# Value casts moved from the transfers to the engines, and a denser first attention, in an attention and gated-MLP kernel

## The chip, the cores and the metric

The kernel runs on one core of a Trainium2 chip. The metric is the device time of one execution in microseconds (us), as a median of several; the time of the kernel before is the median of three executions. The profile is of one execution of the same program, whose span of 335.5 us counts from the first to the last instruction.

The core's engines run side by side, each through its own queue in program order: TensorE (PE in the profile, with its weight loads as PEld), VectorE (DVE), ScalarE (ACT), GpSimd (POOL), and SyncE (SP), which here only issues DMA transfers. GpSimd issues transfers too.

## The reference

Eight heads of attention with a narrow causal mask, then a two-layer gated MLP over the result. The input sizes are 8 batches, 8 heads, 576 positions and 64 dimensions per head; the MLP goes from 512 to 2048 and back to 512.

```python
scores = q @ k.T / 8
# heads 0..3 (plain):   0 <= i - j < 32
# heads 4..7 (dilated): 0 <= i - j < 128 and (i - j) % 4 == 0
attn = softmax(where(mask, scores, -1e9)) @ v

x = attn.transpose(0, 2, 1, 3).reshape(8 * 576, 512)
h = x @ w_in                       # 512 -> 2048
g = h * sigmoid(beta * h)
out = g @ w_out                    # 2048 -> 512
```

All inputs are float32 in device memory, and so is the output; the kernel computes its matmuls in bfloat16.

## The kernel before

The work is a list of named steps, which a static schedule threads between the matmuls of the MLP. The MLP works on nine tiles of 512 tokens; while tile `t` is in work, the attention of batch `t + 1` is spread among its matmuls. Batch 0 has nothing to hide behind: its attention comes first, in the order of the list `FIRST`.

The steps, `x` being a pair of heads (0 and 1 plain, 2 and 3 dilated) and the second digit a part of the sequence:

- `Kx`, `Qx` transpose keys and queries of a pair on TensorE and copy the result from PSUM to SBUF. They are used for batches 0 and 1. From batch 2 on a DMA transpose does this, and `d`, `k`, `q` are the copies that spread its result.
- `Sxj` computes scores, and ScalarE the exp of them into `pt`; `Vxj` multiplies by the values and VectorE divides by the sums into `xs`; `Xxj` transposes that, and ScalarE copies it into `xT`, from which the MLP reads its tokens.
- `vn` brings values into the form with a one behind each row (`vd` for the dilated heads; `vp` holds the plain ones).
- `zn` writes zeros, `Hn` is the first half of an MLP block, and `Wn` is n matmuls of 512 columns on zeros, which compute nothing.

```python
FIRST = (
    "W10 K2 W2 Q2 W2 K3 S20 S21 Q3 W1 S22 S23 z0 S30 S31 S32 S33 v0 W2 V20 V21 K0 v1 W1 V22 K1 V23 W1 Q0 "
    "V30 W1 V31 W1 X20 S00 V32 S01 V33 X21 S02 S10 X30 S11 V00 S12 X31 V01 H0 X00 V10 H1 X01 V11 X10 X11 "
    "z1 z2"
).split()
```

Values come by DMA from GpSimd's queue, which turns float32 into bfloat16 on the way. The plain ones land in place, the dilated ones in a staging tile of two buffers, from which a bfloat16 copy spreads them:

```python
vp = [const([P, 4, NI, DV], BF16, f"vp{i}") for i in range(2)]
vd = [const([P, 2, 4, C, DV], BF16, f"vd{i}") for i in range(2)]
vd_st = [const([P, 2, 4, C * D], BF16, f"vd_st{i}") for i in range(2)]
# ... (cut)
def load_vp(b, eng, n=0, m=4 * NI, p=0):
    st = vp[b % 2][:].rearrange("p h i d -> p (h i) d")
    for e in range(2):
        eng.dma_start(out=st[64 * e + p:64 * e + 64, n:n + m, 0:D], in_=...)   # cut

def spread_v(b, hf, eng):
    K = DK[hf]
    copy_on(eng)(
        out=vd[b % 2][0:K, hf].rearrange("p h T e -> p (h T) e")[:, :, 0:D],
        in_=vd_st[b % 2][0:K, hf].rearrange("p h (T d) -> p (h T) d", T=C))
```

PSUM tiles of the attention rotate over four banks (`at`), and in the first attention every third over the two of `h_ps` as well. A bank is free for its next user when its reader (exp, a copy or a division) is done. The copies of a `Q` step on plain heads, and an MLP block:

```python
for n, hf in ((0, 0), (1, 1), (0, 1), (1, 0)):
    # ... (cut: out is a half of the query tile)
    copy_on(nc.scalar if hf or b == 0 and x == 0 and n else nc.vector)(out=out, in_=tv[n][rows])
# ... (cut)
def slot_h(t, fb, kts=None):
    # ... (cut: PSUM tile)
    for kt in kts or (2, 3, 0, 1):
        nc.tensor.matmul(hps, lhsT=w_in_bf[:, kt, fb * P:(fb + 1) * P],
                         rhs=xT[:, kt, t * NTOK:(t + 1) * NTOK], start=(kt == 2), stop=(kt == 1))
    # ... (cut)
    nc.scalar.activation(out=tnh[:], in_=hps, func=ACT.Tanh, scale=beta_half[:, fb:fb + 1])
    nc.vector.scalar_tensor_tensor(out=g[:], in0=tnh[:], scalar=1.0, in1=hps, op0=ALU.add, op1=ALU.mult)
```

Where each batch's next values are fetched and spread (V is VectorE, A ScalarE, G GpSimd, SQ SyncE's queue; `at(step, ...)` puts the call ahead of that step of batch `b`):

```python
if b == 1:
    at("X20", gate, raw[2, "q"][0:1, 0:1])
    at("X20", load_vp, b + 1, G)
    at("X10", spread_v, b + 1, 0, A)
    at("X11", spread_v, b + 1, 1, A)
if b > 1:
    # ... (cut: cast_qk)
    at("X20", load_vd, b + 1, G)
    at("X20", load_vp, b + 1, G)
    # ... (cut: DMA transposes, spread_dil)
    at("X00", spread_v, b + 1, 0, G)
    at("X01", spread_v, b + 1, 1, G)
```

`gate` is a copy of one element on GpSimd that holds its queue until the last transposed queries of batch 2 are there. GpSimd also multiplies the exps by the masks from batch 2 on.

Of the kernel before, what the change touches and what calls it, by code (L numbers as in the profile page):

```python
# [23 lines left out]
    "W10 K2 W2 Q2 W2 K3 S20 S21 Q3 W1 S22 S23 z0 S30 S31 S32 S33 v0 W2 V20 V21 K0 v1 W1 V22 K1 V23 W1 Q0 "  # L24
    "V30 W1 V31 W1 X20 S00 V32 S01 V33 X21 S02 S10 X30 S11 V00 S12 X31 V01 H0 X00 V10 H1 X01 V11 X10 X11 "
# [3 lines left out]
    "K2 Q2 K3 Q3 v0 S20 S21 v1 S22 S23 K0 K1 S30 V20 S31 Q0 V21 S32 V22 S33 V23 V30 S00 "  # L29
    "V31 X20 S01 V32 S02 V33 S10 X21 S11 V00 X30 S12 V01 X31 V10 X00 V11 X01 X10 X11"  # L30
).split()
THIRD = (
    "d0 d1 S20 S21 S22 k0 S23 V20 S30 k1 V21 S31 q0 V22 S32 q1 V23 S33 q2 q3 V30 X20 S00 V31 "
    "S01 X21 V32 S02 V33 S10 V00 X30 S11 V01 S12 X31 V10 X00 V11 X01 X10 X11"
# [4 lines left out]
def kernel(  # L39
# [83 lines left out]
    vd_st = [const([P, 2, 4, C * D], BF16, f"vd_st{i}") for i in range(2)]  # L123
# [24 lines left out]
    def zeros():  # L148
# [7 lines left out]
        nc.vector.memset(vp[0][0:WIN, 0, 0, 0:D], 0.0)  # L156
# [142 lines left out]
    def load_vp_1(b, eng, n=0, m=4 * NI, p=0):  # L299
        eng.dma_start(  # L300
            out=vp[b % 2][:].rearrange("p h i d -> p (h i) d")[p:P, n:n + m, 0:D],
            in_=bass.AP(tensor=v.tensor, offset=v[b, 0].offset + (QT * n - WIN + p) * D,
                        ap=[[D, P - p], [QT * D, m], [1, D]]))


    def load_vp(b, eng, n=0, m=4 * NI, p=0):
        st = vp[b % 2][:].rearrange("p h i d -> p (h i) d")
        for e in range(2):
            eng.dma_start(
                out=st[64 * e + p:64 * e + 64, n:n + m, 0:D],  # L310
# [4 lines left out]
    def load_vd(b, eng):  # L315
        rows = v[b, 4:8].rearrange("h (t T) d -> t h (T d)", T=C)
        for hf in range(2):
            eng.dma_start(out=vd_st[b % 2][0:DK[hf], hf], in_=rows[DO[hf]:DO[hf] + DK[hf]])  # L318

    def spread_v(b, hf, eng):  # L320
        K = DK[hf]
        copy_on(eng)(  # L322
            out=vd[b % 2][0:K, hf].rearrange("p h T e -> p (h T) e")[:, :, 0:D],
            in_=vd_st[b % 2][0:K, hf].rearrange("p h (T d) -> p (h T) d", T=C))

# [42 lines left out]
    def step_q(b, x):  # L368
        tv = [transposes_p("q", y) for y in (x, x + 1)] if x < 2 else transposes_d("q", x)
        h = slice(2 * (x - 2), 2 * (x - 2) + 2)  # L370
        for n, hf in ((0, 0), (1, 1), (0, 1), (1, 0)):
# [3 lines left out]
            copy_on(nc.scalar if hf or b == 0 and x == 0 and n else nc.vector)(  # L375
# [94 lines left out]
    BRING = {"d": spread_dil, "k": spread_k, "q": spread_q, "v": spread_v, "z": zeros_q}  # L470

    def attention_step(b, name):
# [3 lines left out]
        elif name[0] == "H":  # L476
            early[0] = -1
            slot_h(0, int(name[1:]), (2, 3))
        elif name[0] in STEP:
            STEP[name[0]](b, *[int(c) for c in name[1:]])  # L480
        else:
            BRING[name[0]](b, int(name[1:]), nc.vector)

# [91 lines left out]
    def extras(b):  # L575
# [4 lines left out]
        if b + 1 < B:  # L580
            if b == 1:
                at("X20", gate, raw[2, "q"][0:1, 0:1])
                at("X20", load_vp, b + 1, G)
                at("X10", spread_v, b + 1, 0, A)
                at("X11", spread_v, b + 1, 1, A)
            if b > 1:
                for kind in "kq":
                    at("S20", cast_qk, b + 1, kind)
                at("X20", load_vd, b + 1, G)
                at("X20", load_vp, b + 1, G)  # L590
# [5 lines left out]
            if b > 1:  # L596
                at("S11", spread_dil, b + 1, 0, V)
                at("V01", spread_dil, b + 1, 1, V)
                at("X00", spread_v, b + 1, 0, G)
                at("X01", spread_v, b + 1, 1, G)  # L600
# [23 lines left out]
    build_neg_p()  # L624
    load_vp_1(0, G, 2 * NI, 2 * NI)
    for c0, c1 in ((0, 256), (256, 512), (512, 1024), (1024, 2048)):
        load_w_in(c0, c1)
    make_identity(nc, ident_f[:])
    for name in FIRST:
        if name == "X10":  # L630
            build_beta()
        attention_step(0, name)
    for x, g in ((1, 0), (0, 1)):
        for n in "kq":
            load_tok(1, n, x)
        load_w_out(g)
    load_vd(1, G)
# [8 lines left out]
    load_vd(2, G)  # L646
# [7 lines left out]
    WORK = {"S": 3, "V": 3, "X": 2, "d": 3, "K": 3, "Q": 3, "k": 0, "q": 0, "v": 0}  # L654
# [64 lines left out]
```

The softmax here doesn't subtract the row's maximum and nothing guards it: scores larger than these inputs give would overflow.

## Time and profile before

| what | value |
|---|---|
| time, median of 3 (lowest to highest) | 337.47 us (337.26 to 337.99) |
| span of the profiled execution | 335.5 us, granted TensorE clock 0.99 in the mean |
| first attention up to the first MLP block that runs without a break | 0 to 27.9 us |
| transfers from GpSimd's queue | 37440 packets, 19.66 MB |
| transfers from SyncE's queue | 34224 packets, 16.53 MB |

The profile names engines by the short names given above. A line of a group or of the timeline gives source line, engine, operation, output and inputs by tile name, shapes, and how many; in the timeline the first two numbers are start and duration in us, and square brackets at the end hold the idle time of the engine ahead of the piece and what ended it. The tenths of the page's second part divide the span into 40 slices of 8.4 us, and a digit is the busy share of a slice; `PEclk` is the granted share of TensorE's clock. A busy TensorE is not always one at its peak: at half clock it is busy for twice as long with the same work.

### The profile page before, as it was taken

What the parts mean: (1) busy time and instruction counts of PE and PEld (TensorE: products, weight loads), DVE (VectorE), ACT (ScalarE), POOL (GpSimd) and SP (SyncE); (2) the same over time, 40 slices, a digit from 0 to 9 for tenths busy, and PEclk for the clock granted to TensorE, in tenths of its full rate; (3) what the DMA queues carried; (4) which work ended last, traced back from release to release, by engine and by line L of the source; (5) the groups of instructions that cost most, each with busy time, mean ns of one, the idle gap of its engine ahead of it and who ended that gap; (6) DMA issues with size and microseconds to landing.
All of it is one profiled execution on the core that took longest, in us unless ns stands there. A gap on an engine that the chain in (4) does not pass through costs nothing.

```text
span 335.5 us, 6366 instructions
## 1 busy us (share of the span) xinstructions
PE 317.6 (95%) x2426; PEld 169.1 (50%) x2426; DVE 194.3 (58%) x433; ACT 197.4 (59%) x380; POOL 141.1 (42%) x192
## 2 busy tenths in 40 slices
PE   8898999778799899999999999999999999999995
PEld 3664465434455455555554555555555544444444
DVE  4658765349665775786378637773776344344400
ACT  3577755766556665766566656665666544355511
POOL 8933494324674735564556445743533100000000
PEclk9969999999999999999999999999999999999999
DMA  6999999994949794989489959891011201011132
GB/s 87 172 210 194 201 201 163 153 211 95 114 73 191 128 120 102 158 144 97 84 168 153 98 96 178 139 90 39 25 31 33 60 26 42 32 33 31 31 92 66
DMA packets 71695, 36.60 MB, mean 109 GB/s; under 512 B 55008, under 2 KB 66288, under 8 KB 71280
## 3 DMA queue, kind: packets, MB, share of 16 engines
q0 software_dynamic: 37440, 19.66, 49.2%
q1 hardware_dynamic: 34224, 16.53, 22.8%
q8 instruction: 19, 0.31, 0.4%
q14 instruction: 12, 0.10, 0.1%
HBM read 39.32 MB, written 16.52 MB: 166 GB/s over the span
## 4 chain that ended last, share of the span: by engine, by line
PE 82%; DVE 10%; ACT 4%; DMA 1%; issue 1%; POOL 0%; DVEq 0%; ACTq 0%; POOLq 0%
PE h_ps L496 30%; PE o_ps L534 26%; PE at L534 5%; DVE g L506 4%; PE at L436 4%; PE at L496 3%; PE at L453 3%; ACT tnh L503 2%; PE at L403 2%; DVE qq L293 2%; PE h_ps L534 2%; DVE xs L443 2%; PE at L410 2%; DMA xT<-in_k_dram 1%; PE at L351 1%
## 5 line engine op out<-in xcount | busy, mean ns | idle before, releaser
L506 DVE SCALAR_TENSOR_TENSOR g<-tnh,h_ps 128x512 bf16<-128x512 bf16 x130 | 88.8, 684 | 92.5 <-ACT tnh L503 92.0
L496 PE MATMUL h_ps<-xT,w_in_bf 128*128 128x512 bf16 x520 | 130.9, 379 | 3.8 <-ACT xT L459 2.2
L503 ACT ACTIVATE tnh<-h_ps,beta_half 128x512 bf16<-128x512 f32 x130 | 89.3, 687 | 55.5 <-PE h_ps L496 52.6
L534 PE MATMUL o_ps<-w_out_bf,g 128*128 128x512 bf16 x448 | 112.8, 379 | 0.0
L496 PEld LDWEIGHTS <-w_in_bf 128*128 128x128 bf16 x576 | 51.7, 97 | 53.9 <-issue 5.6
L534 PEld LDWEIGHTS <-g 128*128 128x128 bf16 x560 | 50.4, 97 | 47.6 <-issue 0.2
L418 POOL TENSOR_TENSOR pt<-pt,mask_d 96x384 bf16<-96x384 bf16 (+1 forms) x48 | 37.0, 781 | 56.1 <-ACT pt L416 55.5
L416 ACT ACTIVATE pt<-at 128x384 bf16<-128x384 f32 (+2 forms) x107 | 46.2, 439 | 22.2 <-PE at L403 10.9
L443 DVE TENSOR_TENSOR xs<-at,rcp 48x256 bf16<-48x256 f32 (+2 forms) x91 | 42.1, 463 | 9.1 <-PE at L453 4.9
L418 POOL TENSOR_TENSOR pt<-pt,mask_PP 128x384 bf16<-128x384 bf16 x24 | 22.7, 947 | 33.4 <-ACT pt L416 33.3
L436 PEld LDWEIGHTS <-pt 128*128 128x128 bf16 (+2 forms) x448 | 24.7, 99 | 15.1 <-DVE vd L322 1.7
L539 ACT ACTIVATE osb<-o_ps 128x512 f32<-128x512 f32 x28 | 16.7, 597 | 18.6 <-PE o_ps L534 18.5
L410 PEld LDWEIGHTS <-kdT 128*96 128x96 bf16 (+1 forms) x128 | 14.3, 120 | 11.5 <-issue 2.1
L439 DVE RECIPROCAL rcp<-at 48x4 f32<-48x4 f32 (+2 forms) x91 | 16.0, 176 | 6.0 <-PE at L436 5.2
L534 PE MATMUL at<-w_out_bf,g 128*128 128x512 bf16 x80 | 19.4, 379 | 0.0
L453 PEld LDWEIGHTS <-xs 96*128 96x128 bf16 (+1 forms) x224 | 13.7, 97 | 10.9 <-issue 2.3
L453 PE MATMUL at<-ident_b,xs 96*128 96x96 bf16 (+1 forms) x224 | 18.5, 201 | 0.7 <-ACT xT L459 0.5
L436 PE MATMUL at<-vd,pt 96*128 96x65 bf16 (+1 forms) x244 | 17.6, 195 | 0.9 <-DVE vd L322 0.9
L410 PE MATMUL at<-qzd,kdT 128*80 128x96 bf16 (+1 forms) x122 | 17.1, 226 | 1.4 <-DVE qzd L281 1.4
L403 PE MATMUL at<-qq,kz 128*128 128x96 bf16 x144 | 12.1, 206 | 3.6 <-DVE qq L293 3.6
L318 POOL DMA_DIRECT2D vd_st<-in_v_dram x16 | 11.2, 702 | 10.1 <-DMA w_in_bf<-in_moe_w_in_dram 6.9
L467 ACT COPY xT<-at 128x384 bf16<-128x384 bf16 (+1 forms) x32 | 12.7, 395 | 3.8 <-PE at L453 3.8
(113 smaller groups left out, 269.7 us busy)
## 6 DMA issues: line engine op xcount, KB each, us to landing
qk<-in_k_dram POOLq DMA_DIRECT2D x6, 576.0 KB, 7.3
qk<-in_q_dram POOLq DMA_DIRECT2D x6, 576.0 KB, 10.0
vp<-in_v_dram POOLq DMA_DIRECT2D x13, 192.0 KB, 6.9
w_out_bf<-in_moe_w_out_dram POOLq DMA_DIRECT2D x4, 512.0 KB, 17.2
out_dram<-osb SPq DMA_DIRECT2D x7, 256.0 KB, 2.8
out_dram<-osb SPq DMA_DIRECT2D x8, 224.0 KB, 2.4
vd_st<-in_v_dram POOLq DMA_DIRECT2D x8, 192.0 KB, 4.1
out_dram<-osb SPq DMA_DIRECT2D x8, 192.0 KB, 2.3
```

The costliest lines, as they stand in the source:

```text
L403: nc.tensor.matmul(sc[:, a, h2 * n:(h2 + 1) * n], lhsT=kz[b % 2][:, h4, i].rearrange("p e u -> p (e u)"), rhs=qq[b % 2][:, h4, i].rearrang ...
L410: nc.tensor.matmul(sc[0:K, a, 0:2 * n], lhsT=kd[b][:, rp, h4, DO[hf]:DO[hf] + K], rhs=qzd[b % 2][:, :, rp, h4, hf * DQ[0]:hf * DQ[0] + n], ...
L416: nc.scalar.activation(out=w, in_=sc[0:K, :, 0:2 * n], func=ACT.Exp, scale=SCALE)
L418: nc.gpsimd.tensor_tensor(out=w, in0=w, in1=mask[0:K], op=ALU.mult)
L436: nc.tensor.matmul(pv[:, a, h2, :], lhsT=pt[x][0:K, c:c + P], rhs=rhs, start=True, stop=True)
L443: nc.vector.tensor_tensor(out=xs_t[b, x, jx][:, a0:a0 + m], in0=pv[0:n, :, :, 0:D], in1=rcp[0:n, 0:m].unsqueeze(3).to_broadcast([n, m, 2, ...
L453: nc.tensor.transpose(xp[:, a * n:(a + 1) * n], xs[:, a].rearrange("p h d -> p (h d)"), ident_b[0:n, 0:n])
L496: nc.tensor.matmul(hps, lhsT=w_in_bf[:, kt, fb * P:(fb + 1) * P], rhs=xT[:, kt, t * NTOK:(t + 1) * NTOK], start=(kt == 2), stop=(kt == 1))
L503: nc.scalar.activation(out=tnh[:], in_=hps, func=ACT.Tanh, scale=beta_half[:, fb:fb + 1])
L506: nc.vector.scalar_tensor_tensor(out=g[:], in0=tnh[:], scalar=1.0, in1=hps, op0=ALU.add, op1=ALU.mult)
L534: nc.tensor.matmul(ops[:], lhsT=g_t[t, fb][:, tb * P:(tb + 1) * P], rhs=w_out_bf[:, fb, :], start=(fb == 0), stop=(fb == NFB - 1))
L539: nc.scalar.mul(out=osb[:], in_=ops[:], mul=0.5)
```

## The change

It does three things.

1. Values are no longer cast by the transfer. All of them land as float32 in staging tiles (`vp_st`, `vd_st`, the latter now one buffer), and `cast_v` copies them to bfloat16 on an engine: on VectorE or GpSimd for batch 0, VectorE and ScalarE for batch 1, ScalarE for batch 2, GpSimd from batch 3 on. From batch 2 on their transfers are issued on SyncE's queue.
2. The first attention is put in another order, with fewer `W`: the transposes of plain keys and queries follow each other, the plain scores begin among the second dilated pair's values, and of Q0's four copies VectorE takes two instead of one.
3. GpSimd's queue at the start is rearranged: the mask of the plain scores and the loads of `w_in` come behind the first value cast, the last half of `w_in` behind the cast of the first plain values.

A step `v` also counts in the pacing of steps among the MLP's matmuls now, which moves a few steps by one place in the first two tiles.

```diff
 FIRST = (
-    "... v0 W2 V20 V21 K0 v1 W1 V22 K1 V23 W1 Q0 "
-    "V30 W1 V31 W1 X20 S00 V32 S01 V33 X21 S02 S10 X30 S11 V00 S12 X31 V01 H0 X00 V10 H1 X01 V11 X10 X11 "
+    "... v0 W2 V20 V21 v1 K0 W1 K1 V22 Q0 V23 "
+    "V30 S00 V31 X20 S01 V32 S02 V33 X21 v4 S10 X30 S11 V00 S12 X31 V01 H0 v5 X00 V10 H1 X01 V11 X10 X11 "
 SECOND = (
-    "K2 Q2 K3 Q3 v0 S20 S21 v1 S22 S23 K0 K1 S30 ... V31 X20 S01 V32 ..."
+    "K2 Q2 K3 Q3 v0 S20 v1 S21 S22 S23 K0 K1 S30 ... V31 X20 v2 S01 V32 ..."
 THIRD = (
-    "d0 d1 S20 S21 S22 k0 S23 V20 S30 ... V33 S10 V00 ..."
+    "d0 d1 v0 S20 S21 S22 k0 S23 v1 V20 S30 ... V33 v2 S10 V00 ..."
...
-    vd_st = [const([P, 2, 4, C * D], BF16, f"vd_st{i}") for i in range(2)]
+    vp_st = [const([P, 4, NI, D], FP32, f"vp_st{i}") for i in range(2)]
+    vd_st = const([P, 2, 4, C, D], FP32, "vd_st")
...
-    def spread_v(b, hf, eng):
+    def cast_v(b, n, eng):
+        if n == 2 or n > 3:
+            h = slice(0, 4) if n == 2 else slice(2 * n - 8, 2 * n - 6)
+            copy_on(eng)(out=vp[b % 2][:, h, :, 0:D], in_=vp_st[b % 2][:, h])
+        else:
+            f, K = (slice(n, n + 1), DK[n]) if n < 2 else (slice(0, 2), 96)
+            copy_on(eng)(out=vd[b % 2][0:K, f]...[:, :, 0:D], in_=vd_st[0:K, f]...)
...
-            copy_on(nc.scalar if hf or b == 0 and x == 0 and n else nc.vector)(
+            copy_on(nc.scalar if hf else nc.vector)(
...
-            BRING[name[0]](b, int(name[1:]), nc.vector)
+            eng = (nc.scalar if name[0] == "v" and (b, name) in ((1, "v2"), (2, "v0"), (2, "v1"), (2, "v2")) else
+                   nc.gpsimd if b == 0 and name in ("v1", "v4", "v5") else nc.vector)
+            BRING[name[0]](b, int(name[1:]), eng)
...
-            if b == 1:
-                at("X20", gate, raw[2, "q"][0:1, 0:1])
-                at("X20", load_vp, b + 1, G)
-                at("X10", spread_v, b + 1, 0, A)
-                at("X11", spread_v, b + 1, 1, A)
             if b > 1:
+                if b == 2:
+                    at("S20", gate, raw[2, "q"][0:1, 0:1])
                 ...
-                at("X20", load_vd, b + 1, G)
-                at("X20", load_vp, b + 1, G)
+                at("X20", load_vd, b + 1, SQ)
+                at("X20", load_vp, b + 1, SQ)
+            if b == 1:
+                at("X20", load_vd, b + 1, SQ)
+                at("X20", load_vp, b + 1, SQ)
...
-                at("X00", spread_v, b + 1, 0, G)
-                at("X01", spread_v, b + 1, 1, G)
+                at("X00", cast_v, b + 1, 3, G)
+                at("X01", cast_v, b + 1, 2, G)
...
-    build_neg_p()
     load_vp_1(0, G, 2 * NI, 2 * NI)
-    for c0, c1 in ((0, 256), (256, 512), (512, 1024), (1024, 2048)):
-        load_w_in(c0, c1)
-    make_identity(nc, ident_f[:])
     for name in FIRST:
+        if name == "v1":
+            attention_step(0, "v1")
+            build_neg_p()
+            for c0, c1 in ((0, 256), (256, 512), (512, 1024)):
+                load_w_in(c0, c1)
+            continue
+        if name == "v5":
+            load_w_in(1024, 2048)
+            make_identity(nc, ident_f[:])
...
+    G.memset(vd_st[64:96, 1], 0.0)
     load_vd(1, G)
...
-    load_vd(2, G)
...
-    WORK = {"S": 3, "V": 3, "X": 2, "d": 3, "K": 3, "Q": 3, "k": 0, "q": 0, "v": 0}
+    WORK = {"S": 3, "V": 3, "X": 2, "d": 3, "K": 3, "Q": 3, "k": 0, "q": 0, "v": 1}
```

## The prediction

> **What bounds the kernel now.** I read the page's first two parts first: which engine is busy, and when it is not.
>
> ```profile
> PE 317.6 (95%) x2426; PEld 169.1 (50%) x2426; DVE 194.3 (58%) x433; ACT 197.4 (59%) x380; POOL 141.1 (42%) x192
> PE   8898999778799899999999999999999999999995
> PEclk9969999999999999999999999999999999999999
> ```
>
> TensorE is busy for 317.6 of 335.5 us, no other engine for more than 59%. Of the idle 17.9 us, 3.8 lie behind the last matmuls and all but 0.8 of the rest before 120 us; one slice (16.8 to 25.2 us) had a granted clock of 0.6. The windows of that stretch and of two later ones (PE, PEld, DVE, ACT, POOL busy, clock, DMA share, GB/s):
>
> ```profile
> 12.00:16.00 4.00, 3.10 (x59) 2.13 (x60) 2.90 (x10) 1.28 (x2) 3.53 (x7) 0.91 2.10 162
> 16.00:20.00 4.00, 4.00 (x58) 3.03 (x57) 1.89 (x7) 2.48 (x5) 2.61 (x5) 0.50 1.40 199
> 20.00:24.00 4.00, 3.85 (x44) 2.90 (x43) 1.92 (x8) 3.13 (x9) 1.43 (x2) 0.74 1.16 213
> 60.00:70.00 10.00, 7.92 (x72) 4.32 (x69) 3.96 (x10) 7.63 (x15) 3.14 (x5) 1.00 1.17 167
> 180.00:200.00 20.00, 19.73 (x164) 10.57 (x162) 11.90 (x28) 12.50 (x25) 11.48 (x14) 1.00 0.94 106
> ```
>
> From 120 us on TensorE idles about 0.3 us per batch: three waits of 0.27 us for a query copy on VectorE are all that the timeline lists from 120 us until the last ten. So nothing that the change does to GpSimd or DMA after the third batch can save much, and only a new wait there could cost. What can move lies before 120 us. The timeline of TensorE there has these large stalls:
>
> ```profile
> 67.48 0.38 PE L496 MATMUL h_ps<-xT,w_in_bf 128*128 128x512 bf16 x1 [1.98 <-ACT xT L459]
> 72.68 0.50 PE L410 MATMUL at<-qzd,kdT 128*96 128x192 bf16 x4 [1.37 <-DVE qzd L281]
> 86.00 0.34 PE L403 MATMUL at<-qq,kz 128*128 128x96 bf16 x4 [1.49 <-DVE qq L293]
> ```
>
> What ScalarE did before the first of them:
>
> ```profile
> 64.36 0.60 ACT L539 ACTIVATE osb<-o_ps 128x512 f32<-128x512 f32 x1
> 64.86 1.03 ACT L322 COPY vd<-vd_st 96x1024 bf16<-96x1024 bf16 x1
> 65.79 0.40 ACT L459 COPY xT<-at 128x288 bf16<-128x288 bf16 x1
> 66.08 1.05 ACT L322 COPY vd<-vd_st 80x1024 bf16<-80x1024 bf16 x1
> 67.03 0.40 ACT L459 COPY xT<-at 128x288 bf16<-128x288 bf16 x1
> ```
>
> Two value copies for batch 2 stand in ScalarE's queue ahead of the last two copies into `xT`, and the next token tile's first block needs the last of these. And in the first attention, warm-up matmuls (`W`) that compute nothing stand on the path at half clock, ahead of the first plain scores:
>
> ```profile
> 17.44 0.62 PE L475 MATMUL o_ps<-warm_w 128*128 128x512 bf16 x1
> 17.85 0.43 PE L436 MATMUL at<-vd,pt 96*128 96x65 bf16 x4
> 18.09 0.62 PE L475 MATMUL o_ps<-warm_w 128*128 128x512 bf16 x1
> 18.82 0.52 PE L391 MATMUL h_ps<-neg_p,ident_b 128*128 128x384 bf16 x1
> ```
>
> **What the Trainium skill says.** "TensorE: Matmul & The Clock Gate", Part 1: the clock is gated to half after a quiet window of about 3.4 us and restored after a busy one, with windows that run free of the kernel; Part 4 adds that transposes don't count as busy in the same way. The trace agrees: 0.50 in 16 to 20 us, after four microseconds of transposes and waits, and a 128x384 matmul takes 0.52 us there against 0.33 later. "VectorE: DVE Perf Modes", Mode 2×_2P: a float32 copy within SBUF can run at two elements a cycle, where bf16 gets four. The before trace has only bf16: 96x1024 in 0.35 us undisturbed, about 1.0 while GpSimd worked. "SBUF — State Buffer", Who interferes with whom: such copies and GpSimd shut each other out of a port pair; those 1.0 us fit that. "DMA: Bandwidth & Descriptors", SWDGE vs HWDGE vs iDMA: a cast during the transfer has to be issued from GpSimd. Hence the old loads of values all stand on POOL, at 0.97 us an issue for `vp` and 0.70 for `vd_st`; float32 staging lets batches from the third on use SyncE's queue.
>
> **The change part by part.**
>
> (a) *First attention.* Four single warm-ups after V21 become one. The three that go took 0.43, 0.43 and about 0.41 us on the chain that ended last, 1.27 in all. V22 also loses its 0.49 us wait for the second value copy, since K0, one warm-up and K1 now stand ahead of it. Against that, the first value copy is float32: 1024 elements at 1.92 per ns are 0.53, plus some 0.1 fixed, so 0.62 against 0.35: +0.3. And the first plain scores must wait for query copies that come right behind Q0. With V20 at about 12.5, K0, W, K1, V22 end near 14.5 and Q0's 36 transposes, at half clock 1.5 us, near 16. ScalarE then copies (1,1) and (0,1), 0.64 each, so S00 can start at 17.2, where it was 18.8. V31 and X20 (0.22 + 0.32) are now behind S00 instead of ahead: a lead of 1.1 us at half clock. If the clock comes back at 22.2 as before, work that is 1.1 us ahead in cold time is 0.55 ahead in warm time. I count −0.6 at the start of the MoE tiles.
>
> (b) *Values of heads 0 to 3, batch 0.* They land in float32 and GpSimd casts each half, 768 elements. Its copies ran at about 1.0 ns an element (80x1024 in 1.04 us), so 0.8 us. The loads landed some 7 us after issue: 17 to 18 us, so casts end near 18.5 and 20.5; the first consumer stood at 22.7. Hidden. GpSimd's wait delays the last half of `w_in` by some 4 us in issue, but the DMA engines have a backlog until then, and its first use is past 34 us, against a landing at 28. Hidden: 0.
>
> (c) *Batch 1.* Two VectorE casts stay, in float32, about 1.0 us each as before because GpSimd works beside them: 0. One ScalarE cast of `vp` is new: 0.83 ns an element (597 ns at 512, 385 at 256) and 0.17 fixed, so 1536 elements take 1.45 us, at about 55.5 us where ScalarE is under half busy. S10 needs the bank of S01 some 2.6 us later and the exp then ends about in time: +0.1.
>
> (d) *End of batch 1.* The two copies of 1.03 and 1.05 leave ScalarE's queue. Three `xT` copies then follow the `osb` at 64.96 at 0.30 us spacing and end at 65.9, where TensorE is at the wait from 65.3 on. 1.98 us become about 0.6: −1.4.
>
> (e) *Batch 2.* Its three casts now run on ScalarE inside the second token tile. The first falls into a gap of 1.88 us: free. With the changed pacing both query copies of the dilated heads follow each other on VectorE, where a `g` of 0.60 stood between: −0.6 of the 1.37. The second cast (1.04) stands between two `tnh` in a stretch where VectorE is the tight engine and ScalarE has some 0.4 to spare: +0.5. The third, 1.45, among plain scores with TensorE 99% busy: +0.3.
>
> (f) *Batches 3 to 7.* GpSimd per batch: 2 × 0.97 + 2 × 0.70 + 2.07 = 5.4 us before; 2.05 (2048 elements) + 1.55 (1536) = 3.6 after. It was idle a good part anyway, and TensorE's order there is unchanged: 0.
>
> Sum: −0.6 + 0.1 − 1.4 − 0.6 + 0.5 + 0.3 = −1.7, so 337.5 becomes 335.8 us.
>
> **Rivals.** *First: the clock.* With fewer warm-ups a second quiet window could follow, as S00 waits for the query copies; another 3.4 us at half clock loses 1.7 us, and the gains are gone: 337.5. For it: the window from 12 to 16 was already too quiet with the warm-ups in. Against: from 18.8 on scores, values and transposes stand densely, with no idle, as before. The opposite, a clock that stays up, would save some 2 us more: 333.8. *Second: ScalarE becomes the wait in the second tile.* A `tnh` held up by 1.0 to 1.5 us holds a `g`, and that a bank of `h_ps`, of which there are two. If each of the four new casts shows in full (1.45 + 1.03 + 1.04 + 1.45 = 5.0), less (a), (d) and (e), the time is about 339.9. Against: ScalarE idles for 55.5 us ahead of its `tnh` waiting on matmuls. *Third: late staging.* The loads of batch 2 now sit behind the DMA transposes on SyncE's queue, whose last landed at 61.8; if they land after 71, a cast blocks ScalarE, with exp and `tnh` behind it: +1 to +4. Against: some ten microseconds of slack, and loads of this size landed in 4.1 us at the median. *Fourth: GpSimd's casts block VectorE's copies* in the later batches, up to 3.6 us each, and TensorE's 0.27 waits grow to about 1: +4. Against: the masks' products already run there.
>
> **Range and chances.** The parts are each uncertain by some 0.5 to 1 us and mostly independent: ±2.3. Predicted 335.8, with 333.3 to 338.2 holding 8 times in 10. To be faster by 2% it must lose 6.7 us, half of the 13.3 that all idle time before 120 us adds up to: 4%. Slower by 2% needs the second and fourth rivals at once: 4%. The rest, 92%, within.
>
> **What would show it.** Right: no value copy before the last `xT` copies of batch 1, and the wait at 67.5 under 0.8; S00 near 17.2; the dilated query wait under 0.9; idle from 120 us unchanged. Wrong: a low clock past 23 us; TensorE waits on ScalarE's `vd` or `vp` in the second tile; waits on `qq` over 0.5 us per batch later; ScalarE waiting for `vd_st`.

## The result, and the profile after

| | before | after |
|---|---|---|
| time, median | 337.38 us (4 executions) | 335.81 us (4 executions, 335.19 to 336.29) |
| ratio | | 0.9949, 95% interval 0.9927 to 0.9971 |
| span of the profiled execution | 335.5 us | 334.6 us |
| granted TensorE clock in it | 0.99 | 0.984 |
| transfers on GpSimd's queue | 37440 packets, 19.66 MB | 7632 packets, 16.64 MB |
| transfers on SyncE's queue | 34224 packets, 16.53 MB | 57264 packets, 25.58 MB |

The kernel became 1.6 us faster; 335.8 was predicted. The profile shows that this sum came about in another way than the prediction had it: one step had the wrong sign (the first attention, +1.0 for −0.6), two were put too small (a gain of 2.8 for 1.9, a loss of 0.9 for 0.5), and one that was put at nothing gained 0.7.

The page's first two parts, after (busy time of the engines; 40 slices of 8.4 us):

```profile
PE 318.5 (95%) x2423; PEld 169.6 (51%) x2423; DVE 194.8 (58%) x433; ACT 198.7 (59%) x381; POOL 131.5 (39%) x172
PE   8698999997999899999999999999999999999995
PEclk9959999998999999999999999999999999999999
```

TensorE is busy for 0.9 us more than before, with the same work less three warm-ups: part of what was won in idle time was paid back as time at half clock. The second slice has become emptier (6 where it was 8). The third has a lower clock than before (5, not 6), and there is a new dip in the tenth slice. The windows of the same stretches, after, and one more from 80 us (PE, PEld, DVE, ACT, POOL busy, clock, DMA share, GB/s):

```profile
12.00:16.00 4.00, 1.64 (x40) 1.26 (x41) 1.63 (x5) 0.68 (x2) 2.62 (x5) 1.00 1.19 199
16.00:20.00 4.00, 3.29 (x66) 2.67 (x61) 2.18 (x5) 1.91 (x4) 3.24 (x7) 0.59 1.18 174
20.00:24.00 4.00, 4.00 (x41) 3.20 (x39) 2.44 (x9) 2.76 (x7) 4.00 (x8) 0.55 1.05 160
60.00:70.00 10.00, 9.48 (x83) 5.16 (x81) 5.20 (x13) 7.21 (x16) 1.21 (x3) 1.00 1.14 203
80.00:90.00 10.00, 8.91 (x62) 4.37 (x60) 7.51 (x18) 5.08 (x10) 1.60 (x3) 0.83 0.65 137
```

From 12 to 16 us TensorE was busy for 1.64 us where it had been 3.10. From 60 to 70 us it is the reverse: 9.48 where it had been 7.92. The timeline of TensorE after, at the places that matter (start, duration, what; in brackets the idle time ahead and what ended it):

```profile
14.77 0.65 PE L358 MATMUL h_ps<-ident_b,xT 64*64 64x64 bf16 x18 [1.78 <-DMA xT<-in_k_dram]
19.71 0.48 PE L404 MATMUL at<-qq,xT 128*128 128x192 bf16 x2 [0.38 <-ACT qq L382]
28.75 0.38 PE L505 MATMUL h_ps<-xT,w_in_bf 128*128 128x512 bf16 x1 [0.27 <-ACT xT L466]
65.47 0.30 PE L460 MATMUL at<-ident_b,xs 96*128 96x96 bf16 x3 [0.52 <-DVE xs L450]
70.86 0.50 PE L417 MATMUL at<-qzd,kdT 128*96 128x192 bf16 x4 [0.76 <-DVE qzd L282]
79.46 1.02 PE L505 MATMUL h_ps<-xT,w_in_bf 128*128 128x512 bf16 x4 [1.08 <-DVE g L515]
81.36 1.65 PE L505 MATMUL h_ps<-xT,w_in_bf 128*128 128x512 bf16 x4 [0.75 <-DVE g L515]
115.33 0.34 PE L410 MATMUL at<-qq,kz 128*128 128x96 bf16 x4 [1.30 <-DVE qq L294]
```

The lines of before that go with the first, the sixth and the seventh of these:

```profile
12.82 0.65 PE L351 MATMUL h_ps<-ident_b,xT 64*64 64x64 bf16 x18 [0.23 <-DMA xT<-in_k_dram]
80.74 1.02 PE L496 MATMUL h_ps<-xT,w_in_bf 128*128 128x512 bf16 x4 [0.55 <-DVE g L506]
82.25 1.02 PE L496 MATMUL h_ps<-xT,w_in_bf 128*128 128x512 bf16 x4 [0.36 <-DVE g L506]
```

The first line is the first plain key transpose: its wait for the tokens' own transfer is now 1.78 us, where it was 0.23. The mask of the first plain scores goes in at 18.82, as before, and their product starts at 19.71 (before: 19.14). The 1.98 us for `xT` at 67.48 are gone, with 0.52 for `xs` in their place. The dilated query wait of 1.37 is 0.76. The two waits on a `g` that were 0.55 and 0.36 (at 80.74 and 82.25) are 1.08 and 0.75, and the second of these blocks falls into a stretch at half clock: 1.65 us for four matmuls instead of 1.02.

ScalarE ahead of the place where the 1.98 stood, after:

```profile
64.73 0.60 ACT L548 ACTIVATE osb<-o_ps 128x512 f32<-128x512 f32 x1 [0.47 <-PE o_ps L543]
65.23 1.00 ACT L466 COPY xT<-at 128x288 bf16<-128x288 bf16 x3
```

No value copy stands among the `xT` copies; three of them take 1.00 us together.

**The ledger.** The change was profiled twice (the second time as the repeat below), and one table of start times (us) of the same work shows where the time went:

| place | before | after | after, repeat |
|---|---|---|---|
| first MLP block without a break | 27.73 | 28.75 | 27.73 |
| dilated scores of batch 2 (waits for `qzd`) | 72.68 | 70.86 | 70.63 |
| second of the MLP blocks that wait for a `g` | 82.25 | 81.36 | 81.11 |
| plain scores of batch 3 (wait for `qq`) | 115.56 | 115.33 | 113.93 |
| end | 335.5 | 334.6 | 333.1 |

The differences from row to row are the steps' worths. After: +1.0 in the first attention, −2.8 up to batch 2's dilated scores, +0.9 at the two waits for a `g`, +0.7 from there to batch 3's plain scores, −0.7 after them: −0.9 in all. Repeat: 0, −2.05, +0.9, −0.5, −0.8: −2.4. The two executions of one program differ by 1.5 us: 1.0 in the first attention and 1.2 from 81 us on, less 0.8 the other way between them.

### The profile page after: what moved, and what is told of

The parts are those of the page before. It is cut to its first block, busy times and chain, and to the rows that moved or that the text cites. A ratio compares the mean times of both kernels' runs of the same rounds, so it can differ in the third digit from the quotient of the medians.

```text
span 334.6 us, 6370 instructions
## 1 busy us (share of the span) xinstructions
PE 318.5 (95%) x2423; PEld 169.6 (51%) x2423; DVE 194.8 (58%) x433; ACT 198.7 (59%) x381; POOL 131.5 (39%) x172
## 3 DMA queue, kind: packets, MB, share of 16 engines
q1 hardware_dynamic: 57264, 25.58, 39.8%
q0 software_dynamic: 7632, 16.64, 27.7%
## 4 chain that ended last, share of the span: by engine, by line
PE 84%; DVE 5%; ACT 3%; DMA 3%; POOL 2%; issue 1%; POOLq 0%; ACTq 0%; DVEq 0%
PE h_ps L505 31%; PE o_ps L543 28%; PE at L543 5%; PE at L443 4%; PE at L460 3%; PE at L505 3%; DMA xT<-in_q_dram 3%; DVE g L515 2%; PE at L410 2%; PE h_ps L543 2%; PE at L417 2%; ACT tnh L512 1%; PE at L559 1%; POOL pt L425 1%; DVE xs L450 1%
## 5 line engine op out<-in xcount | busy, mean ns | idle before, releaser
L450 DVE TENSOR_TENSOR xs<-at,rcp 96x256 bf16<-96x256 f32 (+2 forms) x93 | 43.0, 462 | 9.2 <-PE at L460 5.0
L446 DVE RECIPROCAL rcp<-at 96x4 f32<-96x4 f32 (+2 forms) x93 | 16.3, 176 | 8.6 <-PE at L443 8.0
L460 PE MATMUL at<-ident_b,xs 96*128 96x96 bf16 (+1 forms) x220 | 17.8, 201 | 1.5 <-DVE xs L450 1.0
L443 PE MATMUL at<-vd,pt 80*128 80x65 bf16 (+1 forms) x252 | 18.5, 197 | 0.7 <-DVE vd L329 0.7
L417 PE MATMUL at<-qzd,kdT 128*80 128x96 bf16 (+1 forms) x122 | 17.2, 227 | 0.8 <-DVE qzd L282 0.8
L425 POOL TENSOR_TENSOR pt<-pt,mask_FP 128x384 bf16<-128x384 bf16 x12 | 10.9, 911 | 17.0 <-ACT pt L423 17.0
L505 PE MATMUL at<-xT,w_in_bf 128*128 128x512 bf16 x56 | 13.8, 379 | 0.7 <-DVE kdT L371 0.4
L474 ACT COPY xT<-at 128x192 bf16<-128x192 bf16 (+1 forms) x31 | 12.2, 393 | 3.6 <-PE at L460 3.6
```

Source lines behind the costliest of these rows:

```text
L417: nc.tensor.matmul(sc[0:K, a, 0:2 * n], lhsT=kd[b][:, rp, h4, DO[hf]:DO[hf] + K], rhs=qzd[b % 2][:, :, rp, h4, hf * DQ[0]:hf * DQ[0] + n], ...
L425: nc.gpsimd.tensor_tensor(out=w, in0=w, in1=mask[0:K], op=ALU.mult)
L443: nc.tensor.matmul(pv[:, a, h2, :], lhsT=pt[x][0:K, c:c + P], rhs=rhs, start=True, stop=True)
L446: nc.vector.reciprocal(out=rcp[0:n, 0:m], in_=pv[0:n, :, :, D])
L450: nc.vector.tensor_tensor(out=xs_t[b, x, jx][:, a0:a0 + m], in0=pv[0:n, :, :, 0:D], in1=rcp[0:n, 0:m].unsqueeze(3).to_broadcast([n, m, 2, ...
L460: nc.tensor.transpose(xp[:, a * n:(a + 1) * n], xs[:, a].rearrange("p h d -> p (h d)"), ident_b[0:n, 0:n])
```

## The experiments

The kernel before ran beside each of them; its median was 337.0 to 337.2 us every time. Experiments 2, 3, 7 and 8 ran on another chip than the rest; the kernel before took 336.99 us there, and 337.0 and 337.16 on the chip of the others.

**1. The change once more.** No edit.

> The changed kernel once more, unaltered, beside the next three. Theory A (K0's tokens land later and at times that vary from one execution to the next, as float32 values stand ahead of them): K0's start anywhere from 13.6 to 14.8, time 335.4 us, ratio 0.995. Theory B (the profile shown first is typical): K0 at 14.8 again, ratio 0.995.

Measured: 335.59 us (15 executions, 333.75 to 337.67), ratio 0.995 (0.9929 to 0.9972). The same lines of the timeline:

```profile
14.12 0.65 PE L358 MATMUL h_ps<-ident_b,xT 64*64 64x64 bf16 x18 [1.41 <-DMA xT<-in_k_dram]
46.98 1.02 PE L543 MATMUL h_ps<-w_out_bf,g 128*128 128x512 bf16 x4 [0.88 <-DVE g L515]
79.22 1.02 PE L505 MATMUL h_ps<-xT,w_in_bf 128*128 128x512 bf16 x4 [1.09 <-DVE g L515]
```

The token wait is there again and varies with the transfers: 1.41 and 1.78 us. So are the waits for a `g` (1.09, then 0.74), but at 81 us the clock stays up this time. New here is 0.88 us at 46.98, which the first profile doesn't have.

The executions of both kernels fall into groups by their mean granted clock, some 0.005 apart; one stretch of 3.4 us at half clock (the profile after has one from 81.4 to 84.8, clock 0.53) makes 0.005 of a span of 335 us. All executions of the two kernels that ran as or beside experiments, by the mean clock to the nearest 0.005 (mean time, number; two of the kernel before, at 340 us, are left out):

| clock | before | after |
|---|---|---|
| 0.980 | | 336.38 (3) |
| 0.985 | 337.58 (2) | 335.54 (6) |
| 0.990 | 337.50 (74) | 334.52 (6) |
| 0.995 | 336.09 (30) | |
| 1.000 | 335.15 (8) | |

At the one clock where both have some number of executions, 0.990, the change is worth 3.0 us; at 0.985, with only two executions of the kernel before, 2.0. The medians, 335.59 against 337.0, show 1.4. So part of the gain is lost because the changed kernel gets a lower clock more often; how much, 0.6 to 1.6 us by these groups, is not measured more closely, since no experiment sets the clock alone.

**2. The new first attention alone.** The kernel before, with the change's order of steps, its copies of Q0 on two engines, its second value copy on GpSimd and its order of GpSimd's queue (but for the last half of `w_in`, which follows the rest); values are still cast by the transfer.

```diff
-    "... V20 V21 K0 v1 W1 V22 K1 V23 W1 Q0 "
-    "V30 W1 V31 W1 X20 S00 ..."
+    "... V20 V21 v1 K0 W1 K1 V22 Q0 V23 "
+    "V30 S00 V31 X20 S01 ..."
-            copy_on(nc.scalar if hf or b == 0 and x == 0 and n else nc.vector)(
+            copy_on(nc.scalar if hf else nc.vector)(
```

> The kernel before, with the new first attention alone: order, three warm-ups fewer, the copies of Q0, the second value copy on GpSimd ahead of the plain mask and w_in; values still cast by the transfers. Theory A (the order is a gain that float32 staging hides): the first unbroken MLP block at 27.1 instead of 27.7, time 336.8 us. Theory B (the order itself is what costs): 28.7 and 338.4 us. Theory C (fewer warm-ups lengthen the stretch at half clock): half clock past 23 us and 338 us or more.

Measured: 336.38 us (21 executions), ratio 0.9973 (0.9954 to 0.9993). The plain keys' transposes started at 12.68, the product of S00 at 17.30 (17.2 was predicted of the change), and the first unbroken MLP block at 26.52, 1.2 us ahead of the kernel before. So the order does what step (a) said, and more at this place; some of it goes again in a longer wait for a `g` at 45.54 (0.65 us, 0.18 before). What cancels it in the changed kernel comes with the float32 values.

**3. Batch 0's dilated values cast by the transfer again.** The changed kernel; the two loads go as bfloat16 into the same staging tile, through another view of it. VectorE and GpSimd still copy them, from that view.

```diff
+    vd_sb = vd_st[:].rearrange(...).bitcast(BF16)[:, 0:8 * C * D].rearrange(...)   # cut
-        st = vd_st[:].rearrange("p f h T d -> p f h (T d)")
+        st = (vd_st[:] if b else vd_sb).rearrange("p f h T d -> p f h (T d)")
```

> The changed kernel, with batch 0's dilated values alone cast by their transfer again (bf16 staging; everything else as changed). Theory A (the doubled bytes of these values, which stand ahead in the queue, bring K0's tokens 2 us later): K0's transposes start near 12.9 instead of 14.8, the first MLP block that runs without a break near 27.2 instead of 28.8, time 334.2 us. Theory B (the tokens are late for another reason, such as GpSimd's queue or the order of the steps): K0 still near 14.8, time 335.8 us.

Measured: 332.55 us (6 executions), ratio 0.9874 (0.9841 to 0.9906): 3 us below the change, where 1.6 was expected. The key transposes started at 12.55 with no wait for tokens, the unbroken MLP at 26.30, 1.4 and 2.4 us ahead of the change's two profiles. What lies ahead of the tokens in GpSimd's queue makes this difference. What made up the rest of the 3 us was not isolated; three of the six executions had a clock of 1.0, which none of the change's had. The view of transfers issued in the first 12 us (KB, us from issue to landing), before:

```profile
xT<-in_k_dram POOLq DMA_DIRECT2D x1, 288.0 KB, 6.0
vd_st<-in_v_dram POOLq DMA_DIRECT2D x1, 160.0 KB, 6.3
```

and after:

```profile
xT<-in_k_dram POOLq DMA_DIRECT2D x1, 288.0 KB, 7.9
vd_st<-in_v_dram POOLq DMA_DIRECT2D x1, 320.0 KB, 8.1
```

The key tokens' transfer is the same 288 KB in both, and lands 1.9 us later after its issue, because the value loads ahead of it write 384 and 320 KB instead of 192 and 160. In this experiment it landed after 5.6 us.

**4. Tokens ahead of the values.** The changed kernel; the plain tokens' loads are issued before those of batch 0's values.

```diff
-    load_vd(0, G)
-    build_neg_d()
     ... (the plain tokens' loads)
+    load_vd(0, G)
+    build_neg_d()
```

> The changed kernel, with the loads of plain keys' and queries' tokens issued ahead of batch 0's float32 values instead of behind. Theory A (what counts is how many bytes stand ahead of whom in the transfer queue): K0 no longer waits, but the values now land some 2 us later, at 14 to 15, and V20 waits for them where it stood at 12.6, so K0 waits behind V20: no gain, 335.8 us. Theory B (the tokens alone are what is late): 334.0 us.

Measured: 337.71 us (22 executions), ratio 1.0033 (1.0012 to 1.0055). The wait moved to the values: 2.99 us on `vd` ahead of V20, which then started at 14.74. With these bytes the order of the loads can't mend it: whichever comes second is late. It is 1.9 us slower than the theory expected: the clock was 0.985 or less in 20 of 22 executions, and VectorE's first cast for batch 1 (at 47.07 us) waited 1.37 us for its load, with a wait of 1.92 on TensorE behind it.

**5. Seven warm-ups in the token wait.** The changed kernel with `W7` ahead of `K0`.

```diff
-    "... V20 V21 v1 K0 W1 K1 V22 Q0 V23 "
+    "... V20 V21 v1 W7 K0 W1 K1 V22 Q0 V23 "
```

> The changed kernel with seven warm-up matmuls of 512 columns put ahead of the first plain key transposes, where TensorE waited 1.4 to 1.8 us for the tokens. Nothing else changes. Theory A (the window from 12 to 16 us is too quiet, since the tokens land late, and that is what takes the clock down at 16 us): seven cost 1.5 us at full clock, so up to 1.5 of the wait is filled for nothing and the path gets longer by at most 0.3; the clock at 16 to 20 us is then 0.9 or more, the first unbroken MLP block starts at 26.5 instead of 27.7 to 28.7, and the time is about 334.0. Theory B (the clock is taken down by the many transposes and waits after 16 us as well, whatever stands ahead): the half clock only moves, the start stays at 27.7 to 28.7, time 335.6 or up to 0.3 more.

Measured: 333.58 us (4 executions, 333.17 to 334.04), ratio 0.9893 (0.985 to 0.9936). The mean clock was 1.0 in three executions and 0.994 in the profiled one. Its windows:

```profile
12.00:16.00 4.00, 3.29 (x49) 1.81 (x48) 1.96 (x6) 1.01 (x4) 3.39 (x6) 1.00 1.20 195
16.00:20.00 4.00, 3.20 (x80) 2.56 (x75) 2.95 (x8) 2.78 (x7) 2.71 (x6) 1.00 1.26 199
20.00:24.00 4.00, 3.82 (x53) 2.76 (x53) 3.18 (x12) 3.17 (x9) 4.00 (x8) 1.00 1.23 214
```

The clock stays at 1.00 through the stretch that had 0.59 and 0.55. The warm-ups took 1.68 us, just what was waited anyway, and the first unbroken MLP block starts at 26.52: as early as in experiment 2. So 512-column matmuls put ahead of 16 us were enough to hold the clock, whatever came after it, and matmuls that compute nothing won 2.0 us. But idle time in this window is not needed for the clock to fall. In experiments 2 and 3 K0 waits for no tokens, and TensorE was busy for 3.65 and 3.80 of these 4 us, mostly with transposes and products of 65 columns. Experiment 3, and below it experiment 9 (described further down), which has the same first attention:

```profile
12.00:16.00 4.00, 3.80 (x94) 3.13 (x95) 2.57 (x9) 1.98 (x5) 3.37 (x7) 0.90 1.10 229
16.00:20.00 4.00, 3.61 (x32) 2.73 (x31) 2.76 (x10) 2.76 (x6) 3.68 (x8) 0.50 1.34 196
...
12.00:16.00 4.00, 3.60 (x94) 2.92 (x95) 2.56 (x9) 2.06 (x4) 3.43 (x7) 1.00 1.09 231
```

The clock falls in the first and stays at 1.00 in the second, up to 24 us and beyond. With this first attention it can go either way; which mixture of matmuls suffices is not settled.

**6. The three removed warm-ups put back.**

```diff
-    "... V22 Q0 V23 "
-    "V30 S00 V31 X20 ..."
+    "... V22 Q0 W1 V23 "
+    "V30 W1 S00 V31 W1 X20 ..."
```

> The changed kernel with the three single warm-ups put back, where they stood in the kernel before: one behind the first plain query transposes, one ahead of the first plain scores and one behind the third value step of the second dilated pair. Theory A (step (a) of the prediction: they lie on the path at half clock and cost what they take): 3 times 0.42 us is +1.3, of which the later end of the cold stretch gives half back, so +0.6 to +1.3 and a time of 336.2 to 336.9. Theory B (TensorE waits for late tokens and query copies there anyway, so that they fill waits, and they help the clock): 0 or a gain, 335.0 to 335.6.

Measured: 334.73 us (20 executions), ratio 0.9928 (0.9905 to 0.995). They cost nothing that shows: executions at a clock of 0.990 took 334.76 us, against the change's 334.52, and 0.990 is now the commonest clock where it was 0.985 and 0.990 in equal number. Step (a) had booked their removal as 1.27 us off the path. The profile still has a half clock at 16 to 20 us (0.50): all three stand behind 16 us. The intervals of this run and of the change overlap, so that a gain isn't shown, only that the loss of 0.6 to 1.3 us didn't come.

**7. Batch 2's value copies moved, alone.** The kernel before, with its two copies (bfloat16) taken from the end of batch 1 and put, still on ScalarE, where the change has its first and second cast.

```diff
-    "d0 d1 S20 S21 S22 k0 S23 V20 ..."
+    "d0 d1 v0 S20 S21 S22 k0 S23 v1 V20 ..."
-                at("X10", spread_v, b + 1, 0, A)
-                at("X11", spread_v, b + 1, 1, A)
```

> The kernel before, with one thing changed: batch 2's two value copies leave ScalarE's queue ahead of X10 and X11 of batch 1 and stand inside the second token tile, as in the changed kernel. Theory A (this move is where the gain comes from): the wait of 1.98 us at 67.5 falls under 0.6, some 0.5 us comes back in the second tile, time 337.4 - 1.4 = 336.0 us. Theory B (the copies only change place, and the second tile loses as much): 337.4 us. Theory C (nothing comes back): 335.6 us.

Measured: 335.97 us (22 executions), ratio 0.9975 (0.996 to 0.9991). The 1.98 us are gone, and this alone brings the two longer waits for a `g`:

```profile
79.10 1.02 PE L496 MATMUL h_ps<-xT,w_in_bf 128*128 128x512 bf16 x3 [1.08 <-DVE g L506]
80.99 1.02 PE L496 MATMUL h_ps<-xT,w_in_bf 128*128 128x512 bf16 x4 [0.75 <-DVE g L506]
```

They are the same to 0.01 us as in the changed kernel: it is the place of the copies on ScalarE that costs 0.9 us, not float32. The traces point to the way. Behind the second copy an exp comes later on ScalarE, so GpSimd's masks on it come at another time against VectorE's copies, which stand ahead of the `g`. In the kernel before:

```profile
78.11 2.10 POOL L418 TENSOR_TENSOR pt<-pt,mask_d 96x384 bf16<-96x384 bf16 x2 [1.55 <-ACT pt L416]
78.74 0.69 DVE L285 COPY kz<-kpT 64x1536 bf16<-64x1536 bf16 x1
80.61 0.45 DVE L293 COPY qq<-qpT 64x1152 bf16<-64x1152 bf16 x1
```

and in the changed kernel, where experiment 7 is alike (1.03 and 0.84):

```profile
76.82 2.10 POOL L425 TENSOR_TENSOR pt<-pt,mask_d 96x384 bf16<-96x384 bf16 x2 [2.08 <-ACT pt L423]
77.12 1.03 DVE L286 COPY kz<-kpT 64x1536 bf16<-64x1536 bf16 x1
79.33 0.83 DVE L294 COPY qq<-qpT 64x1152 bf16<-64x1152 bf16 x1
```

The two copies are 0.34 and 0.38 us longer, 0.72 of the 0.92 by which the two waits grow. The dilated query wait stayed at 1.37, so its shortening needs another part of the change.

**8. Batch 2's casts on GpSimd.** All three, ahead of the masks of the second tile.

```diff
-    "d0 d1 v0 S20 ... S23 v1 V20 ... V33 v2 S10 ..."
+    "d0 d1 v0 v1 v2 S20 ... S23 V20 ... V33 S10 ..."
-            eng = (nc.scalar if ... (2, "v0"), (2, "v1"), (2, "v2") ...          # cut
-                   nc.gpsimd if b == 0 and name in ("v1", "v4", "v5") else nc.vector)
+            eng = (nc.scalar if ... (b, name) in ((1, "v2"),) else               # cut
+                   nc.gpsimd if b == 0 and name in ("v1", "v4", "v5") or b == 2 and name[0] == "v" else nc.vector)
-                    at("S20", gate, raw[2, "q"][0:1, 0:1])
+                    at("d0", gate, raw[2, "q"][0:1, 0:1])     # and cast_qk of batch 3 likewise
```

> The changed kernel, with batch 2's three casts on GpSimd, ahead of its masks, instead of on ScalarE. Theory A (casts on ScalarE in the second tile cause TensorE's waits of 1.08 and 0.75 us near 80 and the half clock after them): waits under 0.6 each, no third stretch at half clock, mean clock 0.99, time 334.0 us. Theory B (those waits come from VectorE's kz and qq copies that stand behind GpSimd's masks): unchanged, 335.8 us. Theory C (the casts on GpSimd shut out VectorE's copies of the dilated queries): the wait of 0.76 at 70.9 grows to over 1.5, 336.5 us.

Measured: 343.13 us (6 executions), ratio 1.0184 (1.0155 to 1.0213). None of the three theories had this. GpSimd, and TensorE behind it:

```profile
77.58 1.47 POOL L326 CAST vp<-vp_st 128x1536 bf16<-128x1536 f32 x1 [8.11 <-DMA vp_st<-in_v_dram]
79.98 0.35 PE L443 MATMUL at<-vd,pt 96*128 96x65 bf16 x3 [5.97 <-POOL pt L425]
```

The plain values of batch 2 land at 77.5 us only, and with the cast at the head of an in-order queue the masks wait 8.11 us for them. This is the prediction's rival of late staging, seen from the engine that had to wait: the change itself escapes it since it puts that cast late, at `v2`.

**9. Only the two dilated casts on GpSimd.** Experiment 3, with `v0` and `v1` of batch 2 on GpSimd ahead of the masks, and the plain cast left on ScalarE.

```diff
-    "d0 d1 v0 S20 S21 S22 k0 S23 v1 V20 ..."
+    "d0 d1 v0 v1 S20 S21 S22 k0 S23 V20 ..."
-            eng = (nc.scalar if ... (2, "v0"), (2, "v1"), (2, "v2") ...
-                   nc.gpsimd if b == 0 and name in ("v1", "v4", "v5") else nc.vector)
+            eng = (nc.scalar if ... (2, "v2") ...
+                   nc.gpsimd if b == 0 and name in ("v1", "v4", "v5") or b == 2 and name in ("v0", "v1") else nc.vector)
-                    at("S20", gate, raw[2, "q"][0:1, 0:1])
+                    at("d0", gate, raw[2, "q"][0:1, 0:1])     # and cast_qk of batch 3 likewise
```

> The changed kernel, with batch 0's dilated values cast by their transfer (as in the first of these runs), and batch 2's two dilated value casts on GpSimd ahead of its masks; the plain cast of batch 2 stays on ScalarE. Theory A (the second dilated cast on ScalarE adds to TensorE's waits near 77 and 79): they fall from 1.08 and 0.75 to about 0.55 and 0.36, as in the kernel before, and nothing holds up the masks, because these two loads had landed by 69.3: 331.8 us. Theory B (the waits come from VectorE's own copies alone): 332.6 us. Theory C (a cast on GpSimd holds up the masks): a wait of V20 on pt over 1 us, 334 us or more.

Measured: 332.8 us (6 executions), ratio 0.9878 (0.9832 to 0.9925), no better than experiment 3 without it. In the timeline of TensorE the first wait for a `g` is back at its old size, and another has grown:

```profile
68.24 0.50 PE L419 MATMUL at<-qzd,kdT 128*96 128x192 bf16 x4 [1.58 <-DVE qzd L284]
76.29 1.02 PE L507 MATMUL h_ps<-xT,w_in_bf 128*128 128x512 bf16 x4 [0.54 <-DVE g L517]
```

0.54 and 0.35 us instead of 1.08 and 0.75, with the two VectorE copies at 0.69 and 0.45 again: ScalarE's casts there were behind those waits. Which of the two, no run separates; in the timeline it is the second that stands ahead of the exp. But GpSimd's casts run beside VectorE's dilated query copies (1.74 us for two, 0.92 in experiment 3), and that wait goes from 0.97 in experiment 3 to 1.58.

**10. More warm-ups on top.** Experiment 9 with seven more (`W4` after `K0`, `W4` ahead of `Q0`).

```diff
-    "... K0 W1 K1 V22 Q0 V23 "
+    "... K0 W4 K1 V22 W4 Q0 V23 "
```

> The kernel of the run before (batch 0's dilated values cast by transfer, batch 2's dilated casts on GpSimd), with seven more warm-up matmuls among the plain transposes of the first attention (four instead of one behind K0, four ahead of Q0): 7 x 0.22 = 1.5 us of TensorE's time at full clock. Theory A (dense 512-column matmuls there keep the clock up, and 6.8 us at half clock go): 331.8 + 1.5 - 3.0 = 330.3 us, no slice with a clock of 0.5. Theory B (the window is quiet anyway): 331.8 + 1.5 to 3.0 = 333.3 to 334.8 us, half clock as before.

Measured: 332.5 us (6 executions, 331.9 to 332.81), ratio 0.9857 (0.9822 to 0.9891). The clock was 0.998 or 1.0 in every one. Four of experiment 9's six were at 0.995 or more and took 331.5 to 333.2: what the clock brings in the others is used up by the warm-ups, with which the first unbroken MLP block starts at 25.65, where experiment 9's profile, at full clock without them, had 24.20.

**11. Fewer of them.** Experiment 3 with four more.

```diff
-    "... K0 W1 K1 V22 Q0 V23 "
+    "... K0 W3 K1 V22 W2 Q0 V23 "
```

> The changed kernel with the dilated values of batch 0 cast by the transfer again (as in the run that gave 332.55 us), plus four more warm-up matmuls: three instead of one between the first and second plain key transposes and two ahead of the first plain query transposes. Seven more had kept the clock at 0.998 to 1.0 in every execution and cost 1.5 us. Theory A (fewer are enough): clock 0.995 or more, the four cost 0.85 us of 2.2 that a whole half-clock stretch or so is worth, time 331.3 to 331.9. Theory B (four leave the window too quiet in most executions): clock 0.987 as without, time 332.6 to 333.4.

Measured: 332.87 us (4 executions, 332.76 to 332.97), ratio 0.9875 (0.9841 to 0.991). Four are enough for the clock (1.0 in three executions, 0.994 in one), and still no gain over experiment 3, whose executions at 1.0 took 331.9 us: the four cost the 0.9 us that they were counted at. The first theory had the clock right and the time wrong by 1 us.

**12. Later values through GpSimd's queue again.** The changed kernel; the loads of batches 3 to 7 are issued by GpSimd, still as float32.

```diff
-                at("X20", load_vd, b + 1, SQ)
-                at("X20", load_vp, b + 1, SQ)
+                at("X20", load_vd, b + 1, SQ if b == 1 else G)
+                at("X20", load_vp, b + 1, SQ if b == 1 else G)
```

> The changed kernel, but the values of batches 3 to 7 are fetched through GpSimd's queue again, still as float32 and cast there. Theory A (the three waits of 0.27 us for a query copy on VectorE at 147, 180 and 214 us went because GpSimd no longer issues transfers beside that copy): the copy takes 0.7 us again instead of 0.46, the three waits come back, and the time is 0.8 us longer, about 336.4. Theory B (they went because of another spacing of the steps, or because the value copies became GpSimd casts of another length): no such waits, time 335.6.

Measured: 335.34 us (20 executions), ratio 0.9931 (0.9909 to 0.9952). VectorE's fourth query copy of batch 4 in the changed kernel:

```profile
146.14 0.46 DVE L294 COPY qq<-qpT 64x1152 bf16<-64x1152 bf16 x1
```

and in this experiment, with TensorE behind it:

```profile
145.64 0.69 DVE L294 COPY qq<-qpT 64x1152 bf16<-64x1152 bf16 x1
...
146.39 0.34 PE L410 MATMUL at<-qq,kz 128*128 128x96 bf16 x4 [0.26 <-DVE qq L294]
```

The three waits are back (at 146, 180 and 213 us, 0.26 each), as the first theory said, with two transfers being issued on GpSimd (1.43 us from 145.33) beside the copy. The median doesn't show the 0.8 us: 335.34 against 335.59, with intervals that overlap. At a clock of 0.990 the executions took 335.03 (12) against 334.52 (6), at 0.985 336.14 (5) against 335.54 (6): some 0.5 us at equal clock.

## Why the prediction was right, and where it was not

The time fell on the predicted value by luck: errors cancelled. The mechanism of the largest step, (d), was right. By its steps:

**(a), first attention: predicted −0.6, +1.0 and 0 in the two profiles. This step failed.** "With V20 at about 12.5, K0, W, K1, V22 end near 14.5" took K0's tokens to land when they had. They came 1.3 to 2 us later, since twice the bytes stand ahead of them (experiments 2 and 3, which keep the order and take the bytes away, begin the MLP at 26.5 and 26.3). And S00, which was to start at 17.2 "where it was 18.8", had its product at 19.71 and 18.68; 18.8 was the start of its mask, and the product of before stood at 19.14. The float32 cast itself took the estimated 0.62 us. Nor did the three warm-ups lie on the path for 1.27 us: put back, they cost 0.2 at equal clock (experiment 6).

**(b), batch 0's plain values: predicted 0.** The casts were as estimated and hidden. What was missed is that GpSimd's first cast, of the second dilated half, had to wait for the late load too, 2.43 us, and that the cost lies in the bytes on this queue and not in the casts.

**(c), batch 1: predicted +0.1.** ScalarE's cast took 1.48 us and no new wait followed. But "Two VectorE casts stay, in float32, about 1.0 us each as before" holds for one profile and not the other: 0.94 us in the first, 1.71 in the repeat, where it held a `g` and TensorE for 0.88. In the repeat a memset of GpSimd ran from 44.42 to 45.79, and the cast, issued at 44.63, ended at 46.34: 0.55 after the memset. In the kernel before, one ran to 45.35 and the copy issued at 44.62 ended at 45.63. This agrees with the Trainium skill, "SBUF — State Buffer", Who interferes with whom: when a VectorE copy in a two-port mode and GpSimd overlap, the second to issue blocks until the first is done. How long such a cast takes depends on the phase against GpSimd's work, so 1.0 us was no constant. Two waits of before, 0.38 us at 58.58 and 0.18 at 46.28, are not listed after, which with (d) and the query wait of (e) makes −2.6 of the ledger's −2.8; in the repeat the 0.88 gives part of that back, and −2.05 is left.

**(d), end of batch 1: predicted −1.4, right.** 1.98 became 0.52, −1.46, by the named mechanism; experiment 7 shows it alone. (The wait began at 65.5, which is 67.48 less 1.98, and not at 65.3.)

**(e), batch 2: predicted +0.2 in all, measured −0.2 in the repeat and +1.0 in the first profile.** The dilated query wait lost 0.61 (−0.6 predicted). The second cast was mis-sized: +0.9, where +0.5 stood; experiments 7 and 9 put it on the casts' place on ScalarE, and most of it is VectorE's copies beside GpSimd's masks, which the prediction didn't count there. After it, waits of 1.49 and 0.51 gave way to 0.35 and 0.30 in the repeat, with new ones of 0.23 for the third cast (+0.3 predicted) and 0.52: −0.5 in the ledger. The +0.9 and this −0.5 are not independent: the wait of 1.49 ends with a query copy on VectorE, and TensorE, held up ahead of it, now comes later to it. From the dilated scores to that wait's end it took 13.32 us before (72.68 to 86.00) and 13.96 in the repeat (70.63 to 84.59), +0.6. In the first profile a half clock came at that place and made it +0.7.

**(f), later batches: predicted 0, was −0.7 to −0.8.** The prediction had named the three 0.27 us waits, and GpSimd's shorter work, and had not put the two together: VectorE's copy was long while GpSimd issued transfers (0.71, then 0.46 us). Experiment 12 brings both back.

**The rivals.** The first one, the clock, happened, and the sign named for it, a low clock past 23 us, came in the first profile (0.55 from 20 to 24 us); but it didn't eat the whole gain, as there was more to eat: 2 to 3 us at equal clock. The Trainium skill, "TensorE: Matmul & The Clock Gate", Part 1, has windows that run free of the kernel; the spread of one program over clocks from 0.979 to 0.99 fits that, though no trace here shows the windows. The quiet window that the prediction held to be the cause was not idle: TensorE was busy from 12 to 16 us for 3.10 us before, and for 3.80 in experiment 3. That its transposes don't count as busy, which the prediction had also taken from that page, would fit; no run here tests it alone. The second, ScalarE as the wait in the second tile, came in small: 0.9 us with the first two casts, mostly by way of VectorE, and 0.23 with the third. The third, late loads: batch 2's dilated loads landed 6.1 and 7.7 us after issue, not 4.1, and its plain ones 13.8. The two dilated loads landed at 67.1 and 69.3, and their casts began at 69.87 and 74.75: "some ten microseconds of slack" were 2.8 and 5.4. They held, and experiment 8 shows the price where the order relies on the plain values so early. The fourth, GpSimd's casts in the way later, did not happen: no idle time of TensorE is listed from 118 to 325 us.

Left open: why the half clock from 81 us on comes in some executions only. All profiles with the two long waits ahead of it (the change, its repeat, experiments 3 to 7, 11 and 12) are alike there, and only three of them have it: the change and experiments 4 and 5.

## What to carry to other kernels

A cast taken from the transfer to an engine doubles the bytes that the transfer writes: in the part that hides behind nothing, count what stands behind those bytes in the same queue, which may not be the tensor that was changed. Where an engine waits in such a part, a wait can be filled with matmuls that compute nothing, and here it paid where there was a wait: seven inside it won 2.0 us (experiment 5), seven among transposes that waited for nothing won nothing that shows (experiment 10). An engine that is not the bottleneck can still cost time by its phase: here copies put on ScalarE moved GpSimd's work beside VectorE's copies, and TensorE waited for those. Compare two kernels also at equal clock, since half a per cent of clock hides or feigns a gain of this size.

## What had not been expected of the hardware

Moving the issue of transfers off GpSimd made copies on VectorE shorter (0.71 to 0.46 us). Executions of one program come in steps of 0.8 to 1.4 us, which follow the mean clock in steps of 0.005. And the same cast of 96x1024 float32 took 0.62 us alone, and 0.94, 1.52 (experiment 10) or 1.71 us beside memsets on GpSimd, by where in the memset it was issued.
